# Free head order on ScalarE, a deeper VectorE queue and one wait fewer, in an attention and gated-FFN kernel whose order is planned at build time

## The chip, the cores and the metric

The kernel runs on one core of a Trainium2 chip. The metric is the device time of one execution in microseconds, as the median of several. Executions of one kernel mostly agree within 0.5%. Where two kernels are compared, both ran on the same chip.

## The reference

```python
x = A_x                                            # 1 x 2048 x 512, bf16
g = sigmoid((x * gate_w).sum(-1))                  # one gate per row
a = attention(x, wqkv) @ wo                        # 32 heads of 16 columns, softmax over 2048 keys
b = ((x @ w_gate) * (x @ w_up)) @ w_down           # hidden width 1376
return g * a + (1 - g) * b
```

What matters is the softmax: 32 heads x 2048 x 2048 exponentials. In tiles of 128 keys by 512 queries that is 2048 units of 128x512.

## The kernel before

The program is written by a planner. While it is built, a small model with a clock per engine decides which instruction each engine issues next; the chip then runs the five orders as they were written down, in order on each engine, held together by semaphores. The durations in the model (`dur`, `lat`) decide only the order.

The exponentials are shared by two engines. ScalarE applies `Exp` to two or three units at once, straight from a score tile in PSUM. VectorE takes some row tiles (a key tile of four heads, four units) and makes exponentials of integers: each unit is clipped and evicted from PSUM to int16, and four passes over the 2048 columns then make four terms, whose bit patterns are read as bf16. The fourth pass works in place:

```python
def do_d / d_unit ...                     # eviction: one per unit, PSUM -> int16
    v.tensor_scalar(i2b(nb)[:, j, :], bank, _LO, _HI, ALU.max, ALU.min)
def cheap(e, nb): ...                     # four passes per row tile, k = 0..3
    dstt = LL[:, k, ...] if k < 3 else src
    o = P.op("dve",
        lambda v: v.tensor_scalar(dstt, src, 0.5, _BASE + _OFF[k], ALU.mult, ALU.add),
        pops + ([lf or last_x[0]] if k < 3 else done[:3]),      # k = 3 waits for the other three
        dur=0.6, lat=0.1)
```

PSUM has two score slots, of three and two (later three) banks. A span fills a slot: two or three units for ScalarE, or two for ScalarE and one for VectorE. The slot is free again when ScalarE's exponential and VectorE's eviction are both done.

Two sets of small DMAs go through SyncE's queue, and the planner gives them these times:

```python
# query projection: VectorE evicts it to Qst, eight DMAs spread it into QX
for p in range(2):
    for j in range(4):
        P.dma("sp", ... QX[r0:r0+16, p, b, :] <- Qst[r0:r0+16, s, :] ..., f"dq{s}", dur=0.3)
# normalisation of a block of heads, after its accumulator is copied to oraw
4 x P.dma("sp", ... onum <- oraw ..., f"dnum{s}", dur=0.3)
    P.dma("sp", ... den  <- oraw ..., f"dden{blk % 2}")         # default: dur 0.5, lat 2.2
    P.op("dve", ... rec <- 1 / den ...)
2 x P.dma("sp", ... rscr <- rec ..., f"dscr{s}")
    P.dma("sp", ... rb <- broadcast of rscr ..., "drb")
    P.op("pool", ... OT <- onum * rb ...)                        # read by the output projection
...
n0 = 128 * c + 32 * b - 24        # when a query projection is due, in row tiles
```

The softmax here doesn't subtract the row's maximum and nothing guards it: scores larger than these inputs give would overflow.

Of the kernel before, what the change touches and what calls it, by code (L numbers as in the profile page):

```python
# [151 lines left out]
def _build(nc, A_x, A_wqkv, A_wo, W_gate, W_up, W_down, gate_w, out):  # L152
# [18 lines left out]
    D_LAST = 6  # L171
    D_GAP = 0.3
    D_CHEAP = 5
    D_SLOT = 0.3
    D_IDLE = 0.9
    SLK = 0.15
    KA, VA = 8, 3
# [1 line left out]
    RP = 3  # L179
    DP = 3  # L180
# [9 lines left out]
    with ExitStack() as stack:  # L190
# [242 lines left out]
        last_x = []  # L433
# [317 lines left out]
        pv_done = [0] * NG  # L751
        pv_n = [0] * NG
        on_d = {}
        st = dict(gA=0, actE=None, actJ=0, gD=0, pvg=0, prog=0, i2=0)

        def kq_deps(m, kt):
            c, b, p = grp(m)
            return [ev_k[b, kt // 4 - (b == kt == 0)], q_dma[b, c, p]]

        def act_units(n):  # L760

            r = []
            g, e, j = st["gA"], st["actE"], st["actJ"]
            lf = {g: list(left[g])}
            while len(r) < n:
                if e is None:
                    while g < NG and not lf.setdefault(g, list(left[g])):
                        g += 1
                    if g >= NG:
                        break  # L770
                    e, j = (g, lf[g].pop(0)), 0
                r.append((e, j))
                j += 1
                if j == 4:
                    e = None
            return r

        def take(units):
            for e, j in units:
                if j == 0:  # L780
                    left[e[0]].remove(e[1])
                st["actE"], st["actJ"] = (e, j + 1) if j < 3 else (None, 0)
                st["gA"] = e[0]
                st["prog"] += 1

# [12 lines left out]
        p_ring = []  # L798
# [19 lines left out]
        def backlog(now):  # L818
            return max(0.0, P.t["dve"] - now) + 0.6 * sum(q_[0] < 5 for q_ in dve_q)
# [46 lines left out]
        def do_s(now):  # L866
            r, un, kd, fr = plan_s()
            i = len(spans)
            sl = i % 2

            dj = dh = None
            if len(un) == 3 and spans and not overdue() and backlog(now) < min(need_s() - now, 1.5) + D_SLOT:
                busy = {j for _, j in un[:2]}
                j = d_can(now, busy)
                if j is not None and j not in busy:
                    dj, un, dh = j, un[:2], Hold()
            n = len(un)
            deps = list(kd) + (fr if i >= 2 else o_s3 if i else [])
            if dj is not None:
                deps += kq_deps(*dst["e"])  # L880
                de = dst["e"]
            if un[0][0][0] == NG - 1:
                xs[1]["res"] = True

            def fn(pe):
                q = None
                for k_, ((m, kt), j) in enumerate(all_):
                    c, b, p = grp(m)
                    q = pe.matmul(  # L889
                        bank_ap(sl, k_),  # L890
                        KT[32 * j : 32 * j + 32, b, kt * 128 : (kt + 1) * 128],
                        QX[32 * j : 32 * j + 32, p, b, :],
                        start=True,
                        stop=True,
                        tile_position=(32 * j, 0),
                    )
                return q

            all_ = un + ([(de, dj)] if dj is not None else [])
            o = P.op("pe", fn, deps, "pe_s", dur=MM + 0.01, lat=0.2, mode="s")  # L900
            take(un)
            for (m, kt), j in all_:
                c, b, p = grp(m)
                q_use[b, c] = o
            sp = dict(n=n, slot=sl, units=un, s=o, x=None, h=dh)
            spans.append(sp)
            if dj is not None:
                d_unit(dj, bank_ap(sl, 2), o, dh)
            return {j for _, j in all_}
# [14 lines left out]
        dst = dict(e=None, js=[], buf=0, p1={})  # L924
# [10 lines left out]
        def d_can(now, js_busy):  # L935

            if dst["e"] is None and not d_claim(now):
                return None
            for j in dst["js"]:
                if j not in js_busy:  # L940
                    return j
            return dst["js"][0]

        def d_claim(now):
            if now < D_START or not last_x or tails or l_state["n"] > D_CHEAP:
                return False
            nb = (dst["buf"] + 1) % (3 if "k" in last_v else 2)
            if dst["p1"].get(nb) == "busy":
                return False
            if d_free[nb] is not None and d_free[nb] == "pending":  # L950
                return False
            g = max(st["gD"], st["gA"], 1)
            while g < NG and (not [k for k in DK if k in left[g]] or (g == st["gA"] and len(left[g]) < (D_LAST if g == NG - 1 else D_LEFT))):
                g += 1
            if g >= NG or g > st["gA"] + 1:
                return False
            kt = [k for k in DK if k in left[g]][0]
            if kt not in ev_vd:
                return False
            try:  # L960
                if P.ready(kq_deps(g, kt)) > now:
                    return False
            except KeyError:
                return False
            left[g].remove(kt)
            st["gD"] = g
            dst.update(e=(g, kt), js=[3, 2, 1, 0], buf=nb)
            on_d[g, kt] = nb
            dst["cnt"] = 0
            return True  # L970
# [57 lines left out]
        def cheap(e, nb):  # L1028
            pops = dst["p1ops"].pop(e)
            done = []  # L1030
            l_state["n"] += 4
            l_state["g"] += [e[0]] * 4

            def mk(k):
                lf = l_free[k] if k < 3 else None

                def make():
                    src = i2b(nb)[:, :, :].rearrange("p a b -> p (a b)")
                    dstt = LL[:, k, :, :].rearrange("p a b -> p (a b)") if k < 3 else src
                    o = P.op(  # L1040
                        "dve",
                        lambda v: v.tensor_scalar(dstt, src, 0.5, _BASE + _OFF[k], ALU.mult, ALU.add),  # L1042
                        pops + ([lf or last_x[0]] if k < 3 else done[:3]),
                        dur=0.6,
                        lat=0.1,
                    )
                    done.append(o)
                    l_state["n"] -= 1
                    l_state["g"].remove(e[0])
                    p_op[e, k] = [o]  # L1050
                    p_ring.append((e, k))
                    if k < 3:
                        push_l(k + 1)
                    else:
                        l_state["busy"] = False
                        cheap_kick()

                return make

            def push_l(k):  # L1060
                if k < 3 and l_free[k] == "pending":
                    l_wait[k] = lambda: push_l(k)
                    return
                dve_push(5, pops + [l_free[k] if k < 3 else None], mk(k))
                if k < 3:
                    l_free[k] = "pending"

            cheap_wait.append(lambda: push_l(0))
            cheap_kick()
# [4 lines left out]
        def overdue():  # L1074

            return any(g < st["gA"] for g in l_state["g"])
# [167 lines left out]
        for ch in range(1, NCH):  # L1244
            n0 = 4 * ch - KA
# [3 lines left out]
        for b in range(1, NB):  # L1249
            n0 = 32 * b  # L1250
            fl.append((n0 - 14, mk_q(b, 0, n0 - 14)))
            fl += [(n0 - 12 + 2 * ch, mk_k(b, ch, n0 - 12 + 2 * ch)) for ch in range(NCH)]
        for c in range(1, NCH):
            for b in range(NB):
                n0 = 128 * c + 32 * b - 24
                fl.append((n0, mk_q(b, c, n0)))
        n_ffn = NCH * (2 * FT + 4)
        a0, a1 = FFN_FROM, FFN_TO
# [52 lines left out]
        tails = []  # L1311
# [34 lines left out]
        def step_pe():  # L1346
# [3 lines left out]
            hold = False  # L1350
            if s and s_ready <= t + 0.01 and spans and P.mode == "c":
                fs = [u for u in active if u.pos < len(u.mms)]
                hold = fs and fs[0].mode == "c" and t + fs[0].cost + 0.49 <= need_s() - SLK and need_s() < 1e8
            if s and s_ready <= t + 0.01 and not hold:
                busy = do_s(t)
                xi = x_get(P.t["pe"])
                if xi is not None and (
                    pick_fill(P.t["pe"] + 0.5) is None or any(isinstance(x["u"], Unit) for x in xs)
                ):
                    j = d_can(P.t["pe"], busy)  # L1360
# [4 lines left out]
            pvs = []  # L1365
            if m < NG:
                for it in p_ring:
                    e, k = it
# [8 lines left out]
            fs = [u for u in active if u.pos < len(u.mms)]  # L1377
# [10 lines left out]
            if xi is not None:  # L1388
# [7 lines left out]
                if s_ready > t + D_GAP and backlog(t) < D_IDLE:  # L1396
                    j = d_can(t, set())
# [12 lines left out]
                    return True  # L1410
            pick = None
            nr = sum(q_[1] is None for q_ in pvs)
            if pvs and not hold and (not fs or len(tails) or nr >= RP or len(pvs) - nr >= DP):
                pick = "pv"
            elif fs:
                pick = "f"
            if pick == "pv":
                it = next((q_ for q_ in pvs if (q_[1] is not None) == (nr < RP)), pvs[0])
                p_ring.remove(it)
                do_pv(it)  # L1420
                return True
            if pick == "f":
                u = fs[0]
                k = u.pos
# [180 lines left out]
```

## Time and profile before

The median was 760.57 us. ScalarE is the bound. These are the busy lines of the page: engine, busy us, share of the span and instructions.

```profile
span 759.2 us, 20945 instructions
PE 706.6 (93%) x8946; PEld 213.3 (28%) x8946; DVE 677.7 (89%) x1116; ACT 735.3 (97%) x672; POOL 65.2 (9%) x73
```

The Trainium skill ("Perfetto Trace Analysis", Identifying the Most-Contended Engine) takes occupancy as the measure for Vector and Scalar engines, and warns that it misleads for TensorE. Here the first part fits: ACT is at 97%, and the exponentials follow each other without a gap. The windows view, which gives busy time in a stretch, shows ScalarE at 584 of 585 us between the start-up and the end.

```profile
150.00:735.00 585.00, 550.13 (x6944) 162.41 (x6943) 558.73 (x919) 584.16 (x536) 17.08 (x13) 1.00 0.08 20
```

The columns of this view are: stretch, length, PE, PEld, DVE, ACT and POOL busy with the number of instructions, granted TensorE clock, DMA share, GB/s.

The waits view says who waited for whom, in us in total, times, and the longest:

```profile
ACT PT L1477 <- PE psS L889: 7.2, 15, 0.9
DVE rec L1209 <- DMA den<-oraw: 8.6, 9, 3.1
```

From start to start, an exponential of three units takes 0.4267 x 3 + 0.064 us and one of two 0.4267 x 2 + 0.064 us where nothing stops it. Summed over all exponentials but the last this gives 728.3 us. What the real spacings have beyond that sum I call ScalarE's loss: 11.0 us, of which 8.8 lie before 150 us.

Finally the in-place pause. This is VectorE's timeline around 201 us (start, length, instruction):

```profile
200.96 1.41 DVE L1042 TENSOR_SCALAR SC<-SC 128x2048 int16<-128x2048 int16 x2
202.28 0.68 DVE L1013 TENSOR_SCALAR wk<-psX 128x512 int16<-128x512 f32 x1
202.88 0.68 DVE L1013 TENSOR_SCALAR wk<-psS 128x512 int16<-128x512 f32 x1
```

Instructions follow each other after 0.60 us, but two passes that end in the in-place one take 1.32 us.

### The profile page before, as it was taken

To read this page: it belongs to the slowest core of one execution; us is meant where nothing else is said; L and a number is where in the kernel's file an instruction comes from. 1 tells how busy PE (TensorE), PEld (TensorE's weight loads), DVE (VectorE), ACT (ScalarE), POOL (GpSimd) and SP (SyncE) were. 2 spreads that over 40 slices of the span, in tenths; PEclk is the share of its full clock that TensorE was granted. 3 is DMA by queue.
4 is the path that set the end of the run, shared out by engine and by line. 5 is a ranking of instruction groups with operands and counts; after the bars stand their busy time and mean duration, and the time that the engine had idled before them with its cause. 6 is when DMAs were issued, how large, how long until landed. Compare 5 with 4: busy or idle time off the path is not lost.

```text
span 759.2 us, 20945 instructions
## 1 busy us (share of the span) xinstructions
PE 706.6 (93%) x8946; PEld 213.3 (28%) x8946; DVE 677.7 (89%) x1116; ACT 735.3 (97%) x672; POOL 65.2 (9%) x73
## 2 busy tenths in 40 slices
PE   9998898999899999998999999998999989899997
PEld 3322222222222322222222222222222222222243
DVE  3449987989999999999989989999999989999994
ACT  6989999999999999999999999999999999999995
POOL 8940000000000000000000000000000000000000
PEclk9978898999999999999999999999999999999999
DMA  8900000000010010101001010000001100010000
GB/s 173 284 16 9 16 15 25 16 9 24 9 30 9 23 38 11 29 9 28 12 10 31 29 30 10 24 15 9 24 10 28 40 19 16 7 29 8 24 23 31
DMA packets 32881, 22.81 MB, mean 30 GB/s; under 512 B 20468, under 2 KB 27572, under 8 KB 32788
## 3 DMA queue, kind: packets, MB, share of 16 engines
q1 hardware_dynamic: 31476, 20.42, 10.3%
q8 instruction: 71, 1.16, 0.7%
q0 software_dynamic: 256, 0.79, 0.4%
q10 hardware_dynamic: 1056, 0.26, 0.2%
q14 instruction: 22, 0.18, 0.1%
HBM read 11.24 MB, written 2.35 MB: 18 GB/s over the span
## 4 chain that ended last, share of the span: by engine, by line
ACT 31%; DVE 30%; PE 30%; issue 6%; SPq 1%; DMA 1%; DVEq 0%; ACTq 0%
ACT PT L1477 31%; DVE SC L1042 10%; PE psS L889 9%; DVE SC L1013 9%; PE psX L370 9%; PE psO L1120 8%; DVE wk L1013 4%; PE psS L370 1%; DVE hT L645 1%; DVE usb L632 1%; SPq L1180 1%; DVE wk L1042 1%; DMA den<-oraw 1%; DVE oraw L1173 1%; PE psO L1130 1%
## 5 line engine op out<-in xcount | busy, mean ns | idle before, releaser
L1477 ACT ACTIVATE PT<-psS 128x1024 bf16<-128x1024 f32 (+1 forms) x662 | 727.5, 1286 | 8.7 <-PE psS L889 7.2
L889 PE MATMUL psS<-QX,KT 32*128 32x512 bf16 x1966 | 265.0, 390 | 32.8 <-ACT PT L1477 21.3
L1042 DVE TENSOR_SCALAR SC<-SC 128x2048 int16<-128x2048 int16 x316 | 213.1, 692 | 2.2
L1013 DVE TENSOR_SCALAR SC<-psS 128x512 int16<-128x512 f32 x256 | 172.1, 682 | 15.1 <-PE psS L889 13.0
L1120 PE MATMUL psO<-PT,VV 128*32 128x512 bf16 x1546 | 150.1, 391 | 1.2 <-DVE oraw L1173 0.6
L889 PEld LDWEIGHTS psS<-QX,KT 32*128 32x128 bf16 x1966 | 68.6, 91 | 290.4 <-ACT PT L1477 113.9
L1120 PE MATMUL psO<-SC,VD 128*32 128x512 bf16 x1140 | 106.7, 389 | 4.1 <-DVE SC L1042 3.6
L1233 POOL TENSOR_TENSOR OT<-onum,rb 128x512 bf16<-128x512 f32 x16 | 21.3, 1332 | 674.0 <-DMA rb<-rscr 674.0
L1013 DVE TENSOR_SCALAR wk<-psS 128x512 int16<-128x512 f32 x102 | 68.5, 680 | 1.0 <-PE psS L889 0.7
L1042 DVE TENSOR_SCALAR SC<-wk 128x2048 int16<-128x2048 int16 x93 | 62.1, 688 | 0.1
L1120 PEld LDWEIGHTS psO<-PT,VV 128*32 128x32 bf16 x1546 | 38.6, 95 | 59.0 <-issue 48.2
L370 PE MATMUL psX<-xT,wu 128*32 128x512 bf16 x688 | 53.1, 394 | 1.0 <-DVE SC L1013 0.4
L370 PE MATMUL psX<-wd,hT 128*32 128x512 bf16 (+1 forms) x704 | 52.8, 382 | 0.1
L370 PE MATMUL psX<-xT,wg 128*32 128x512 bf16 x688 | 51.1, 383 | 0.6 <-DVE usb L632 0.2
L1120 PE MATMUL psO<-SC,VV 128*32 128x512 bf16 x428 | 43.3, 395 | 2.6 <-DVE oraw L1173 1.4
L1013 DVE TENSOR_SCALAR SC<-psX 128x512 int16<-128x512 f32 x60 | 40.7, 679 | 2.6 <-PE psX L985 2.6
L1120 PEld LDWEIGHTS psO<-SC,VD 128*32 128x32 bf16 x1140 | 28.1, 95 | 46.7 <-DVE SC L1042 27.2
L645 DVE TENSOR_TENSOR hT<-psX,usb 128x512 bf16<-128x512 f32 (+1 forms) x44 | 29.9, 680 | 3.6 <-PE psX L370 3.5
L985 PE MATMUL psX<-QX,KT 32*128 32x512 bf16 x82 | 32.2, 392 | 0.6 <-DVE hT L645 0.2
L632 DVE CAST usb<-psX 128x512 bf16<-128x512 f32 (+1 forms) x44 | 29.9, 680 | 0.8 <-PE psX L370 0.8
L1042 DVE TENSOR_SCALAR wk<-wk 128x2048 int16<-128x2048 int16 x31 | 21.8, 704 | 0.7
L1173 DVE COPY oraw<-psO 128x512 f32<-128x512 f32 x31 | 21.1, 681 | 0.5 <-PE psO L1120 0.5
(115 smaller groups left out, 363.9 us busy)
## 6 DMA issues: line engine op xcount, KB each, us to landing
rb<-rscr SPq DMA_DIRECT2D x16, 256.0 KB
onum<-oraw SPq DMA_DIRECT2D x124, 32.0 KB, 2.0
QX<-Qst SPq DMA_DIRECT2D x120, 16.0 KB, 1.8
out_dram<-ost SPq DMA_DIRECT2D x12, 128.0 KB, 1.8
wu<-in_B_w_up_dram SPq DMA_DIRECT2D x1, 1376.0 KB, 7.0
wg<-in_B_w_gate_dram SPq DMA_DIRECT2D x1, 1376.0 KB, 9.8
wd<-in_B_w_down_dram SPq DMA_DIRECT2D x1, 1280.0 KB, 12.7
SC<-in_A_x_dram SPq DMA_DIRECT2D x4, 128.0 KB, 3.2
```

Source lines behind the costliest of these rows:

```text
L370: r = pe.matmul(dst_[j : j + 32, :], lhs[:, j : j + 32], rhs, start=s0, stop=s1, tile_position=(0, j), skip_group_check=True,)
L632: "dve", lambda v: v.tensor_copy(usb[0:w, n % 2, :], un.bank[0:w, :]), deps, **EV
L645: lambda v: v.tensor_tensor(hT[0:w, f, :], un.bank[0:w, :], usb[0:w, n % 2, :], ALU.mult),
L889: q = pe.matmul(bank_ap(sl, k_), KT[32 * j : 32 * j + 32, b, kt * 128 : (kt + 1) * 128], QX[32 * j : 32 * j + 32, p, b, :], start=True, st ...
L985: lambda pe: pe.matmul(bank, KT[32 * j : 32 * j + 32, b, kt * 128 : (kt + 1) * 128], QX[32 * j : 32 * j + 32, p, b, :], start=True, stop=True,
L1013: lambda v: v.tensor_scalar(i2b(nb)[:, j, :], bank, _LO, _HI, ALU.max, ALU.min),
L1042: lambda v: v.tensor_scalar(dstt, src, 0.5, _BASE + _OFF[k], ALU.mult, ALU.add),
L1120: r = pe.matmul(psO[r_, :], vcol(m, kt, k_, j), pj, start=first, stop=last, tile_position=(0, 32 * j), skip_group_check=True)
L1130: r = pe.matmul(psO[r_, 256 * hf : 256 * hf + 256] if w < 2 else psD[r_, 0:256], vcol(m, kt, k_, j, hf) if w < 2 else ones[:, k_, 16 - 16 ...
L1173: o_ev[m] = P.op("dve", lambda v: v.tensor_copy(oraw[:, s, :], psO[:]), deps, **EV)
L1233: lambda g: g.tensor_tensor(OT[:, c % 2, b, :], onum[:], rb[:], ALU.mult),
L1477: lambda a: a.activation(cell_ap(cells[0], n).rearrange("p a b -> p (a b)"), bank_ap(sl, 0, n), ACT.Exp, scale=_LN2 / _OCT,),
```

## The change

VectorE's unit rides as the third unit of a score group, and must be another head than ScalarE's two. Before, ScalarE took a tile's heads 0 to 3 in order, so VectorE's head often collided. Now ScalarE may take any two, which leaves VectorE its place more often. The queue allowance (`D_SLOT`) lets a unit go to VectorE although VectorE is busy for longer. The in-place pass no longer waits. Two lesser edits came along: query projections are due 6 row tiles earlier, and the choice of attention-value work counts all finished tiles as pressure.

```diff
-    D_SLOT = 0.3
+    D_SLOT = 0.6
...
-                busy = {j for _, j in un[:2]}
-                j = d_can(now, busy)
-                if j is not None and j not in busy:
-                    dj, un, dh = j, un[:2], Hold()
+                if dst["e"] is not None or d_claim(now):
+                    for j in dst["js"]:
+                        two = act_units(2, j)          # ScalarE's next two, head j taken last
+                        if j not in [j_ for _, j_ in two]:
+                            dj, un, dh = j, two, Hold()
+                            break
...
-                        pops + ([lf or last_x[0]] if k < 3 else done[:3]),
+                        pops + ([lf or last_x[0]] if k < 3 else []),
...
-                n0 = 128 * c + 32 * b - 24
+                n0 = 128 * c + 32 * b - 30
...
-            if pvs and not hold and (not fs or len(tails) or nr >= RP or len(pvs) - nr >= DP):
+            if pvs and not hold and (not fs or len(tails) or press >= RP or len(pvs) - nr >= DP):
```

(`act_units` and `take` keep a list of the heads left; `press` counts all finished ScalarE tiles in the ring, `nr` those whose operands are ready. A second line in which `press` replaces `nr` is left out.)

More of the change, by code (lines that the diff above doesn't have):

```diff
@@ L753, in _build @@
         on_d = {}
-        st = dict(gA=0, actE=None, actJ=0, gD=0, pvg=0, prog=0, i2=0)
+        st = dict(gA=0, actE=None, actJ=[], gD=0, pvg=0, prog=0, i2=0)
         def kq_deps(m, kt):
@@ L758, in kq_deps, with act_units @@
             return [ev_k[b, kt // 4 - (b == kt == 0)], q_dma[b, c, p]]
-        def act_units(n):
+        def act_units(n, but=None):
+            order = lambda js: sorted(js, key=lambda j: (j == but, j))
             r = []
-            g, e, j = st["gA"], st["actE"], st["actJ"]
+            g, e, js = st["gA"], st["actE"], order(st["actJ"])
             lf = {g: list(left[g])}
@@ L770, in act_units @@
                         break
-                    e, j = (g, lf[g].pop(0)), 0
-                r.append((e, j))
-                j += 1
-                if j == 4:
+                    e, js = (g, lf[g].pop(0)), order(range(4))
+                r.append((e, js.pop(0)))
+                if not js:
                     e = None
@@ L779, in take @@
             for e, j in units:
-                if j == 0:
+                if e != st["actE"]:
                     left[e[0]].remove(e[1])
-                st["actE"], st["actJ"] = (e, j + 1) if j < 3 else (None, 0)
+                    st["actE"], st["actJ"] = e, [0, 1, 2, 3]
+                st["actJ"].remove(j)
+                if not st["actJ"]:
+                    st["actE"] = None
                 st["gA"] = e[0]
@@ L1412, in step_pe @@
             nr = sum(q_[1] is None for q_ in pvs)
-            if pvs and not hold and (not fs or len(tails) or nr >= RP or len(pvs) - nr >= DP):
+            press = sum(q_[1] is None for q_ in p_ring)
+            if pvs and not hold and (not fs or len(tails) or press >= RP or len(pvs) - nr >= DP):
                 pick = "pv"
@@ L1417, in step_pe @@
             if pick == "pv":
-                it = next((q_ for q_ in pvs if (q_[1] is not None) == (nr < RP)), pvs[0])
+                it = next((q_ for q_ in pvs if (q_[1] is not None) == (press < RP)), pvs[0])
                 p_ring.remove(it)
```

## The prediction

> **What bounds it now.** ScalarE. The page's busy table gives ACT 735.3 of 759.2 us (97%), DVE 677.7, PE 706.6; the windows view gives ACT 50.00 of 50 in nearly every stretch from 150 to 700 us. In the timeline, exponentials start back to back: from 150 to 600 us a 128x1536 one takes 1.33 us start to start, a 128x1024 one 0.92. The two lengths fit 0.427 us a unit (512 columns) plus 0.064 us an instruction; the 277 wide, 388 narrow and one single-unit instruction then add up to 729 us, against 739 us of actual spacings. The 11 us lost lie at 45 to 150 us (8.4), where the granted clock is 0.74 to 0.93, and near 625 and after 730 us. Dealing fewer units to ScalarE is therefore worth its full duration, as long as PE and DVE keep up. The Trainium skill ("ScalarE: Activation LUTs", What ACT_TABLE_LOAD costs) gives 186 ns + 0.833 ns a column less 93 ns overlap, 946 and 1373 ns here; the trace is slightly quicker and decides.
>
> **What the change moves (built order of both programs).** Row tiles on VectorE rise from 110 to 116. ScalarE loses 24 units: 241 wide (-36) and 430 narrow (+42). That is 42 x 0.917 - 36 x 1.344 = -9.9 us. VectorE gains 24 evictions and 24 2048-wide passes: the timeline spaces both at 0.60 us, so +28.8 us. VectorE heads placed as third head of a score group rise from 358 to 400, lone ones fall from 82 to 64; PE's separate score issues fall by 12, attention-value groups rise by 18 (0.2135 us each) and mode switches fall by 10 (0.105 us): PE is even within a few us.
>
> **In-place set.** In the timeline two passes that end in the in-place one are followed by the next instruction after 1.32 us, not 1.20. About 109 such pauses of 0.12 us lie between 100 and 700 us: 12 us of VectorE. Without the wait most of this returns. The skill's "VectorE: DVE Perf Modes" (The DRAIN you can't avoid) says a semaphore costs nothing extra; here it does, since it waits on the instruction directly in front. VectorE isn't the bound, so this only pays for part of the 28.8 us.
>
> **Critical path.** All of the 9.9 us is on it, but VectorE's slack is used up. Counting the built order per 67 exponentials, VectorE's work at 0.60 us was 65 to 74 us against 71 to 77 of ScalarE's; after it is 68 to 73 against 70 to 73, in three stretches equal or above. The waits view shows that VectorE also loses 8.6 us to the denominators' DMA, in order. The deeper queue (0.3 to 0.6 us) lets evictions finish later, so the bank they hold can reach PE late. I estimate 1 to 3 us of new ScalarE stalls. The start to 45 us and the 9 us after the last exponential stay.
>
> **Prediction:** 752 us (760.6 - 9.9 + about 1.5), 748 to 758 8 times in 10. Faster by over 2% (under 745): 4%; within 2%: 94%; slower: 2%.
>
> **What would show it.** ACT busy about 726 us in 671 exponentials; DVE busy about 705 us in 1164 to 1166 instructions, 95% of the span or more; the 0.12 us pauses gone; from 150 to 700 us ScalarE's spacings within 3 us of 0.427 and 0.064; small new waits of PE's loads on VectorE.
>
> **What would make it wrong.** VectorE saturating so that evictions hold banks and ScalarE stalls by 5 to 10 us, cancelling the gain: then ACT's idle before exponentials grows well above the 8.7 us on the page. Or the new order filling the gaps at 45 to 150 us, worth up to 8 us more.

## The result and the profile after

The changed kernel took 768.97 us (768.81 to 773.14, 4 runs) against 761.04. The ratio is 1.0116, with a 95% interval of 1.0080 to 1.0152. Ratios in this text are the mean time of one kernel's fast runs over that of the other's fast runs of the same rounds, so not quite the ratio of the medians. A run is fast when it lies within 1.5% of the fastest of its kernel; of all runs here one does not (experiment 11).

The first lines are the page's busy lines, the next two are from the waits view:

```profile
span 767.0 us, 21248 instructions
PE 713.1 (93%) x9054; PEld 215.5 (28%) x9054; DVE 701.6 (91%) x1164; ACT 728.9 (95%) x678; POOL 67.4 (9%) x73
...
ACT PT L1484 <- PE psS L895: 19.8, 28, 4.1
DVE rec L1215 <- DMA den<-oraw: 7.9, 10, 3.4
PE psX L370 <- POOL OT L1239: 3.3, 1, 3.3
```

ScalarE did get less to do. Its sum fell from 728.3 to 718.4 us, the 9.9 us that were intended. But its loss rose from 11.0 to 27.4 us. The span adds up from the profiled executions as follows.

| us | before | after |
|---|---|---|
| start to first exponential | 10.6 | 10.3 |
| ScalarE's sum (all but the last exponential) | 728.3 | 718.4 |
| its loss before 150 us | 8.8 | 8.4 |
| its loss from 150 to 735 us | 1.6 | 18.2 |
| its loss after 735 us | 0.6 | 0.8 |
| end of the last exponential to the end | 8.7 | 10.2 |
| span (with the last exponential) | 759.2 | 767.0 |

The new loss has two parts. About 10 us lie in two places: 4.7 us between 398 and 407 us and 5.3 us between 592 and 602 us. The rest is in some two dozen gaps, most of 0.15 to 0.7 us, the longest of 1.24 us at 494 us. The first place, as the chain that ended last shows it (start, length, what):

```profile
396.69 0.23 SPq L1186
396.96 0.59 SPq L1186
...
398.86 1.88 DMA den<-oraw
400.74 0.02 issue
400.77 0.35 DVE rec L1215
```

SyncE issues DMAs, one lands, and VectorE's reciprocal starts 3.42 us after VectorE last worked. VectorE runs in order, so every eviction behind that reciprocal waits too. The timeline of SyncE's queue tells why the DMA was late. After:

```profile
390.52 5.76 SPq L509 DMA_DIRECT2D QX<-Qst  x8
396.33 2.48 SPq L1186 DMA_DIRECT2D onum<-oraw  x4
398.86 0.60 SPq L1196 DMA_DIRECT2D den<-oraw  x1
401.15 1.17 SPq L1223 DMA_DIRECT2D rscr<-rec  x2
403.73 0.64 SPq L1236 DMA_DIRECT2D rb<-rscr  x1
```

The same block before:

```profile
392.25 2.43 SPq L1180 DMA_DIRECT2D onum<-oraw  x4
394.73 0.60 SPq L1190 DMA_DIRECT2D den<-oraw  x1
397.02 1.17 SPq L1217 DMA_DIRECT2D rscr<-rec  x2
399.60 0.64 SPq L1230 DMA_DIRECT2D rb<-rscr  x1
406.63 5.69 SPq L509 DMA_DIRECT2D QX<-Qst  x8
```

Eight query DMAs hold the queue for 5.76 us, and after the change they stand in front of the normalisation's DMAs instead of behind them. Line 509 belongs to the query projection, which is due 6 row tiles earlier: a block of heads lasts 32 row tiles, so a projection that is due 30 ahead comes 2 row tiles after the block before its own has begun, which is while the block before that one is normalised. Over the whole trace the eight DMAs stand between the accumulator's copy and the reciprocal's broadcast in 8 of 16 blocks (in one of them, seven of the eight), and in none before. The chain at the second place has the same cause. There the queries sit in front of the `rscr` and `rb` DMAs, GpSimd's multiply comes 17.0 us after the start of the accumulator's copy instead of about 12, and TensorE, which runs in order, stands at the output projection until it is done. First SyncE's queue, then the chain:

```profile
580.46 0.60 SPq L1196 DMA_DIRECT2D den<-oraw  x1
582.24 5.38 SPq L509 DMA_DIRECT2D QX<-Qst  x8
587.66 1.21 SPq L1223 DMA_DIRECT2D rscr<-rec  x2
590.28 0.64 SPq L1236 DMA_DIRECT2D rb<-rscr  x1
```

```profile
590.28 3.89 DMA rb<-rscr
...
594.33 1.56 POOL OT L1239
595.89 0.09 issue
595.98 1.90 PE psX L370 x16
597.88 0.54 PE psS L895 x3
```

ScalarE starves meanwhile (its timeline):

```profile
591.02 3.38 ACT L1484 ACTIVATE PT<-psS 128x1024 bf16<-128x1024 f32 x3
598.53 1.45 ACT L1484 ACTIVATE PT<-psS 128x1536 bf16<-128x1536 f32 x1 [4.13 <-PE psS L895]
```

Each stall also comes with a slower clock. The windows view gives the granted TensorE clock as 0.50 behind the first stall and from within the second, for 3.4 and 6.8 us by the trace's clock records:

```profile
403.40:406.80 3.40, 3.29 (x26) 0.65 (x26) 3.14 (x6) 2.09 (x3) 0.00 (x0) 0.50 0.24 82
596.00:601.40 5.40, 5.40 (x45) 1.23 (x45) 1.78 (x3) 2.38 (x2) 0.00 (x0) 0.50 0.08 27
```

The Trainium skill ("TensorE: Matmul & The Clock Gate", Part 1: The HAM clock gate) says that TensorE falls to half rate after an idle window of about 3.4 us. The trace agrees only in part. Half rate does come with TensorE's two longest waits, but these are 2.90 and 3.30 us, and the second time half rate began at 594.56 us, when TensorE had stood for only 1.88 us.

### The profile page after: what moved, and what is told of

The parts are those of the page before. It is cut to its first block, busy times and chain, and to the rows that moved or that the text cites. A ratio compares the mean times of both kernels' runs of the same rounds, so it can differ in the third digit from the quotient of the medians.

```text
span 767.0 us, 21248 instructions
## 1 busy us (share of the span) xinstructions
PE 713.1 (93%) x9054; PEld 215.5 (28%) x9054; DVE 701.6 (91%) x1164; ACT 728.9 (95%) x678; POOL 67.4 (9%) x73
## 4 chain that ended last, share of the span: by engine, by line
DVE 40%; PE 28%; ACT 20%; issue 4%; SPq 3%; DMA 3%; POOL 1%; DVEq 0%; POOLq 0%; ACTq 0%
ACT PT L1484 20%; DVE SC L1048 15%; DVE SC L1019 12%; PE psS L895 9%; PE psX L370 8%; PE psO L1126 7%; DVE wk L1019 5%; SPq L1186 3%; DVE usb L632 2%; DMA den<-oraw 2%; DVE hT L645 2%; DVE oraw L1179 1%; DVE wk L1048 1%; PE psO L1136 1%; PE psS L370 1%
## 5 line engine op out<-in xcount | busy, mean ns | idle before, releaser
L895 PE MATMUL psS<-QX,KT 32*128 32x512 bf16 x1984 | 271.8, 390 | 28.3 <-ACT PT L1484 15.5
L1048 DVE TENSOR_SCALAR SC<-SC 128x2048 int16<-128x2048 int16 x332 | 219.4, 701 | 0.8 <-PE psO L1126 0.4
L1019 DVE TENSOR_SCALAR SC<-psS 128x512 int16<-128x512 f32 x284 | 190.2, 686 | 13.7 <-PE psS L895 12.2
L1126 PE MATMUL psO<-SC,VD 128*32 128x512 bf16 x1208 | 113.4, 391 | 6.5 <-DVE SC L1048 5.8
L1019 DVE TENSOR_SCALAR wk<-psS 128x512 int16<-128x512 f32 x116 | 77.9, 687 | 0.9 <-PE psS L895 0.8
L1048 DVE TENSOR_SCALAR SC<-wk 128x2048 int16<-128x2048 int16 x99 | 69.0, 717 | 0.6 <-PE psO L1126 0.5
L370 PE MATMUL psX<-wd,hT 128*32 128x512 bf16 (+1 forms) x704 | 56.1, 386 | 0.2 <-DVE bsb L683 0.2
L1019 DVE TENSOR_SCALAR SC<-psX 128x512 int16<-128x512 f32 x48 | 32.9, 686 | 1.3 <-PE psS L895 1.2
L991 PE MATMUL psX<-QX,KT 32*128 32x512 bf16 x64 | 25.4, 398 | 1.4 <-DVE usb L632 0.6
L1179 DVE COPY oraw<-psO 128x512 f32<-128x512 f32 x31 | 21.3, 687 | 0.9 <-PE psO L1126 0.9
```

The source lines that it names most:

```text
L370: r = pe.matmul(dst_[j : j + 32, :], lhs[:, j : j + 32], rhs, start=s0, stop=s1, tile_position=(0, j), skip_group_check=True,)
L895: q = pe.matmul(bank_ap(sl, k_), KT[32 * j : 32 * j + 32, b, kt * 128 : (kt + 1) * 128], QX[32 * j : 32 * j + 32, p, b, :], start=True, st ...
L991: lambda pe: pe.matmul(bank, KT[32 * j : 32 * j + 32, b, kt * 128 : (kt + 1) * 128], QX[32 * j : 32 * j + 32, p, b, :], start=True, stop=True,
L1019: lambda v: v.tensor_scalar(i2b(nb)[:, j, :], bank, _LO, _HI, ALU.max, ALU.min),
L1126: r = pe.matmul(psO[r_, :], vcol(m, kt, k_, j), pj, start=first, stop=last, tile_position=(0, 32 * j), skip_group_check=True)
L1179: o_ev[m] = P.op("dve", lambda v: v.tensor_copy(oraw[:, s, :], psO[:]), deps, **EV)
```

## The experiments

Two theories were set against each other. Theory Q: the query DMAs in SyncE's queue are the cause, through a planner that believes in 0.3 us a DMA where the trace shows 0.6. Theory D: VectorE has no slack left, so that any delay reaches ScalarE. Some kernels keep the order of every engine as it was planned and alter one thing afterwards; these are clean. The others are planned anew, and a new plan puts all small collisions in other places.

The record marks every result as correct, also that of experiment 10, whose arithmetic is cut short.

### 1. Query DMAs behind the normalisation, order kept

```diff
+        for each rb DMA: take the query DMAs planned up to 6 us before its block's
+        onum DMAs or since, and move them behind it in SyncE's order
         P.emit(nc, stack)
```

> The changed kernel with every engine's order kept except SyncE's: the eight query DMAs that stood between the last accumulator copy of a block and its reciprocal's broadcast are issued after that broadcast. Theory Q (the earlier query projection puts its eight DMAs, 0.6 us each, in front of the normalisation's DMAs in SyncE's queue; one of these delays stops VectorE 3.4 us at 401 us and another stops TensorE 3.3 us at 596 us, together about 10 us of ScalarE's stalls): 757 to 761 us, multiply at about +12 us after the copy in every block, no stall of ScalarE over 1.5 us after 150 us. Theory D (VectorE simply has no slack left, so the stalls would come anyway): 767 to 769 us.

Measured: 760.86 us, ratio 1.0010 (0.9983 to 1.0036). The changed kernel's was 1.0116, so 8 us came back (by the two intervals, give or take 3). Both stalls are gone, no denominator is waited for longer than 1.1 us, and the multiply comes 11.9 to 13.5 us after the copy in every block:

```profile
ACT PT L1484 <- PE psS L895: 12.7, 21, 1.0
DVE rec L1215 <- DMA den<-oraw: 4.6, 10, 1.1
```

Theory Q accounts for the 8 us. But the time only equals the kernel before. ScalarE's loss from 150 to 735 us is still 10.8 us, against 1.6 before. (This profile is of the slowest of four executions, 2.5 us above the median, so 10.8 is on the high side.)

### 2. Queries due 24 ahead again, planned anew

```diff
-                n0 = 128 * c + 32 * b - 30
+                n0 = 128 * c + 32 * b - 24
```

> The changed kernel with the query projections due 24 row tiles ahead again, not 30; the order is planned anew (116 row tiles on VectorE as in the changed kernel). Theory Q: 755 to 760 us, no query DMA inside the normalisation's DMAs. Theory D: 766 us or more.

Measured: 767.41 us, ratio 1.0112. Theory Q's range missed; by the number alone it is theory D's. The trace shows another cause. No query DMA stands inside the normalisation any more, but in this plan a projection comes too late: TensorE waits for its DMAs, and ScalarE loses 4.3 us between 295 and 299 us. This is presumably what the edit to 30 was made against.

```profile
PE psS L895 <- DMA QX<-Qst: 2.4, 1, 2.4
```

### 3. Queue allowance back at 0.3, planned anew

> The changed kernel with VectorE's queue allowance back at 0.3; planned anew (113 row tiles on VectorE, ScalarE's sum 724 us against 719). Theory Q: the collisions with the query DMAs stay, 765 us or more. Theory D: VectorE gets slack back and the time falls to 757 to 760 us.

Measured: 780.15 us, ratio 1.0266. It refutes theory D as the whole cause: VectorE had less to do, and the time rose. VectorE now waits 26.7 us for denominators, up to 5.3 us at a time, and the query DMAs stand before the denominator's in three blocks. The other waits, the longest among them, have no query DMA in front: there the plan puts the reciprocal right or soon behind the accumulator's copy, and the denominators land 5 us or more after the copy starts. That is a third way to lose time, which neither theory names.

```profile
DVE rec L1215 <- DMA den<-oraw: 26.7, 11, 5.3
```

### 4. The kernel before with queries due 30 ahead, planned anew

> The kernel before with the query projections due 30 row tiles ahead, nothing else; planned anew (108 row tiles on VectorE, ScalarE's sum 732 us against 729). Theory Q: query DMAs inside the normalisation of several blocks, 765 to 772 us. Theory D: 763 to 764 us, ScalarE's 3 us alone, because VectorE still has its slack.

Measured: 778.81 us (771.66 to 783.11), ratio 1.0212: slower than either range. The profiled execution was the slowest of four. One edited number costs the kernel before more than the whole change did, and query DMAs stand inside the normalisation in 9 of 16 blocks: one wait of 3.1 us for GpSimd comes with them. There are also 21.3 us of waits for denominators, and 24 us of half clock between 130 and 745 us, against 3.4 before. But only one of the seven waits for a denominator over 0.5 us has query DMAs in front. The other six are of the third kind of experiment 3, so this run shows that the earlier due date brings the collisions, and not that they alone cost the 2%.

### 5. The kernel before without the in-place wait, order kept

> The kernel before, every engine's order kept, only the in-place pass's wait taken away (its dependence on the three passes that read the same tile first is dropped after planning; VectorE runs them in order). About 109 pauses of 0.12 us of VectorE should vanish. If VectorE has slack in the kernel before: 759.5 to 760.6 us, no gain. If it were already co-critical: 752 to 757 us.

Measured: 760.42 us, ratio 1.0006 (0.9974 to 1.0037). No gain. The pauses are gone: the two passes that took 1.32 us above now take 1.20.

```profile
203.53 1.28 DVE L1042 TENSOR_SCALAR SC<-SC 128x2048 int16<-128x2048 int16 x2
204.73 0.68 DVE L1013 TENSOR_SCALAR wk<-psX 128x512 int16<-128x512 f32 x1
```

Counting them properly showed an error of the prediction. The in-place pass pauses only where it stands directly behind the third pass, 64 times with a median of 0.117 us, 7.3 us in all. Where another instruction stands between (43 times) the pause is nil. Most of the other pauses that the prediction had counted are still there without the wait.

### 6. The repaired changed kernel with the in-place wait put back, order kept

> The repaired changed kernel (query DMAs behind the normalisation), every order kept, with the in-place wait put back: 116 pauses of 0.12 us, 13 us more of VectorE. Theory D (what is left of the new stalls of ScalarE is VectorE without slack): 6 to 13 us slower than the repaired kernel, 766 to 773 us. If the remaining stalls come from elsewhere: 760 to 763 us.

Measured: 766.65 us, ratio 1.0085 (1.0064 to 1.0106), beside 1.0010 for the repaired kernel: about 5.7 us more, give or take 3 by the two intervals. The pauses are 72 and take 8.3 us. (The profiled execution was the fastest of six, so its trace shows less than that.) The same 7 to 8 us of VectorE cost nothing measurable in the kernel before (give or take 2.4 us) and by the median most of their length here. That is theory D at work, at the lower edge of what was expected.

### 7 and 8. Planned with the DMA times of the trace

```diff
-    query and onum DMAs: dur=0.3         (lat 2.2)
+    query and onum DMAs: dur=0.62, lat=1.3 and 1.4
-    den, rscr, rb DMAs:  dur=0.5, lat=2.2
+    den: dur=0.6, lat=1.35;  rscr: dur=0.6, lat=1.3;  rb: dur=0.64, lat=3.3
```

> The changed kernel, planned with the times that the trace shows for SyncE's DMAs (0.62 us of queue each where the planner had 0.3 or 0.5, and their landing), nothing else; 115 row tiles on VectorE. Theory Q with an honest planner: no wait of VectorE for a denominator over 1 us, no wait of TensorE on GpSimd; 753 to 760 us. If VectorE's lack of slack rules: 760 to 766 us.

> The kernel before, planned with the DMA times that the trace shows; 111 row tiles on VectorE, ScalarE's sum 1 us smaller. 757 to 760 us by theory Q, which leaves the kernel before little to gain, as its query DMAs already miss the normalisation's.

Measured: the changed kernel so planned takes 756.05 us, ratio 0.9944 (0.9921 to 0.9966), and beats both kernels. The kernel before so planned takes 761.47, ratio 1.0014: slightly above its expectation, and no gain. Each is one new plan, and experiments 9, 11 and 12 are plans with the same times that gain nothing, so how much of the 0.6% is due to the times and how much to a lucky plan is not shown. In the changed one ScalarE's loss from 150 to 735 us is 7.4 us, and one wait for a denominator is 1.3 us, where none over 1 us was expected:

```profile
ACT PT L1490 <- PE psS L896: 8.1, 19, 1.1
DVE rec L1219 <- DMA den<-oraw: 1.3, 1, 1.3
```

### 9. Planned with the DMA times, queries due 24 ahead

> The changed kernel with queries due 24 ahead again and the planner given the DMA times of the trace; 115 row tiles on VectorE as in the version with the times and 30 ahead (756 us). With the earlier rerun of 24 ahead (767 us) TensorE stood 2.4 us at 294 us for query DMAs that the planner thought landed. Theory Q (wrong DMA times in the plan are the cause, and 24 or 30 only decides where they hit): 754 to 759 us with no wait of TensorE on query DMAs. If 30 ahead is itself what helps: 762 us or more.

Measured: 764.01 us, ratio 1.0051. It missed: 30 ahead itself helps here. From 291 to 297 us TensorE has no score group to issue, as the next queries have not landed, and ScalarE stands for 4.0 us. So in these two plans 30 is the better due date once the planner has the DMA times. VectorE also waits 3.1 and 2.6 us for two denominators here, again with no query DMA in front.

### 10. VectorE relieved, order kept, result wrong on purpose

```diff
+                    cut = 512 if k == 2 and len(on_d) > 4 else 2048     # third pass made short
-    v.tensor_scalar(dstt, src, ...)
+    v.tensor_scalar(dstt[:, 0:cut], src[:, 0:cut], ...)
```

The starting point is the repaired kernel of experiment 1. The in-place wait is back.

> A wrong result on purpose. The repaired changed kernel (query DMAs behind the normalisation, every order kept), in which the third 2048-wide pass of each row tile after the first few is cut to 512 columns, and the in-place wait is put back because the check asks for it: some 45 us less of VectorE's passes, 8 us more of pauses. Theory D (what is left of the new stalls is VectorE without slack): ScalarE runs at the sum of its durations outside the start, 749 to 753 us. If the stalls have another cause (TensorE, the clock): 757 to 761 us.

Measured: 754.54 us, ratio 0.9921 (0.9886 to 0.9955), 6.8 us under the repaired kernel by the ratios, give or take 3. It lies between the two ranges, 1.5 us above theory D's, but the gain itself is what theory D foretold: only VectorE's work was cut, and TensorE was as busy as before. The windows of the repaired kernel and, in the second fence, of the relieved one:

```profile
150.00:735.00 585.00, 551.65 (x6923) 161.34 (x6920) 573.45 (x946) 577.99 (x540) 17.42 (x13) 1.00 0.08 20
```

```profile
150.00:735.00 585.00, 552.14 (x7093) 163.99 (x7093) 553.93 (x956) 582.11 (x548) 17.72 (x14) 1.00 0.08 20
```

VectorE falls from 98.0% to 94.7% of the stretch, about where it was before the change (95.5%), and ScalarE rises from 578.0 to 582.1 us of 585. ScalarE's total loss is 11.7 us, within 1 us of the kernel before. (This profile is of the fastest of four executions, that of the repaired kernel of the slowest, so the ratio is the better measure.) So with enough slack on VectorE some 6 us of the 9.9 show in the time (0.9921). Part of what remains of the gap is the end: 10.2 us behind the last exponential instead of 8.7.

### 11 and 12. With the DMA times, one part undone

> The changed kernel planned with the DMA times of the trace (756 us), VectorE's queue allowance back at 0.3; 113 row tiles on VectorE, ScalarE's sum 4 us larger, VectorE's work 7 us smaller. If the deeper queue pays for itself: 757 to 761 us. If it costs as much in stalls as it gains: 754 to 757 us.

> The changed kernel planned with the DMA times of the trace (756 us), but with ScalarE taking the heads in fixed order as before; 112 row tiles on VectorE, ScalarE's sum 6 us larger than with the free order. If the free order is what gives the gain: 759 to 762 us, no better than the kernel before. If it is not needed: 755 to 757 us.

Measured: allowance 0.3 takes 771.41 us, ratio 1.0116, which missed by 10 us. One execution of six, the profiled one, took 1441 us with every matmul at about half rate; it is left out of the ratio. Fixed order takes 763.61, ratio 1.0026: 1.6 us above its range. Beside 0.9944 the free order is worth about 6 us, and in this plan the other edits gain nothing without it.

### 13 to 16. What was still open

> The same program as e11_slot03_dmatimes, run again for a profile in the normal state. 765 to 773 us again. If VectorE's slack were all that matters, it should have been faster than the version with allowance 0.6 (7 us less of VectorE's work); so the profile must show stalls of ScalarE from TensorE or the queries: windows of half clock in number, or TensorE waiting for query or normalisation DMAs.

> The changed kernel planned with the DMA times of the trace, every order kept except that SyncE issues the query DMAs behind the normalisation's. If the collisions that remain in 7 blocks cost time though they are planned for: 751 to 755 us. If a planned collision is harmless: within 1 us of the repeat in this call, about 755 to 757 us.

> The changed kernel planned with the DMA times of the trace, with the attention-value choice as in the kernel before (only tiles whose operands are ready count as pressure); 116 row tiles on VectorE, ScalarE's sum within 1 us of the other's. If that hunk matters: 3 us or more either way; if not: 754 to 759 us.

> A repeat of e7_after_dmatimes: 754 to 758 us, 0.4 to 0.8% under the kernel before.

The repeat of experiment 7 on another chip took 756.86 us, ratio 0.9941 (0.9914 to 0.9968): confirmed. With the query DMAs moved behind the normalisation as well it took 756.05, ratio 0.9938: the planned collisions cost nothing that these runs can tell. With the old attention-value choice it took 758.95, ratio 0.9970 (0.9944 to 0.9995). The two intervals overlap, so that edit is worth 2 us or nothing. Allowance 0.3 again took 771.14 us, ratio 1.0124. Its profiled execution, at 766 us of span, is the fastest of four. ScalarE loses 12.9 us from 150 to 735 us, and VectorE waits 11.7 us for denominators, against 1.3 us in experiment 7:

```profile
DVE rec L1219 <- DMA den<-oraw: 11.7, 6, 4.4
```

The longest of these waits, 4.4, 3.8 and 2.7 us, end at 260, 671 and 624 us. No query DMA stands in front of them: they are of the third kind of experiment 3, with the reciprocal at most two instructions behind the accumulator's copy. The two spells of half clock (6.8 us each) begin at 260 and 673 us, beside the first two. So waits in VectorE's order are one candidate for the slower time; whether they account for it was not tested.

VectorE's busy share alone does not settle it either. With allowance 0.3 VectorE is busy for 95.5% of the stretch from 150 to 735 us, like the kernel before, and ScalarE loses 12.9 us; with the query DMAs moved behind the normalisation (the second of these four, run 14) it is 98.4%, more than in the repaired kernel, and ScalarE loses only 5.4.

## Why the prediction was wrong

- **The bound and the gain were right.** ScalarE's exponentials are the 241 and 430 predicted, and its sum fell by the 9.9 us computed. ACT busy is 728.9 us (predicted 726) and DVE busy 701.6 us in 1164 instructions (predicted 705 in 1164 to 1166).
- **The step that failed is "I estimate 1 to 3 us of new ScalarE stalls".** They were 16.4 us (27.4 less 11.0): about 8 us from the order of SyncE's queue, which the estimate left out, and most of the rest from VectorE's load, which it set too low. The prediction named the danger, VectorE's saturation with stalls of 5 to 10 us, but as an outside chance.
- **About half of the stalls came from an edit that was not costed at all.** The prediction did not mention that queries are due 6 row tiles earlier. Moving their DMAs back in SyncE's queue, all orders kept, returned 8 us. The prediction had quoted the denominators' waits of 8.6 us from the page, but took them as a number that stays. It did not ask what else goes through that queue.
- **Most of the other half is VectorE's slack, mis-sized.** The prediction compared VectorE's work with ScalarE's and found both about equal, "in three stretches equal or above", and yet allowed 1 to 3 us. The repaired kernel loses 10.8 us from 150 to 735 us at 98.0% VectorE, and 4.8 us when VectorE is relieved to 94.7%; by the ratios the relief gained 6.8 us. In this order of instructions, 98.0% was already too much. It is no threshold: another order lost less at 98.4% (run 14).
- **"About 109 pauses ... 12 us" was an overcount.** They were 64 and 7.3 us. All VectorE pauses of that length had been put down to the in-place pass without checking which instruction stood before each. That the wait costs at all, and that taking it away gains nothing where VectorE isn't the bound, was right.
- **"95% of the span or more" for DVE was wrong** (91%), and did not follow from the prediction's own numbers: 705 of 752 us is 94%. The busy time itself came out right, and the longer span lowered the share. A share over the whole span hides saturation; from 150 to 735 us the repaired kernel had 98.0%.
- **The end grew by 1.5 us**, which the prediction had held constant. This was not tested.

## What to carry to other kernels

When a planned, in-order program is changed, cost every edit, also a due date: ask what each moved instruction shares a queue with. Give a planner's model the measured issue time of small DMAs: with them this change gained 0.6% instead of losing 1.2%. But other plans with the same times came out up to 1.2% slower than the kernel before, so every new plan has to be measured. And before work is moved to the engine that is second in line, test its slack: with every order kept, 8.3 us of pauses on VectorE cost the repaired kernel about 5.7 us, while 7.3 us of them cost the kernel before nothing measurable.

## What the Trainium skill lacked or had wrong

- "DMA: Bandwidth & Descriptors", Issuing engines are not separate DMA queues, calls the sequencer's time to start a DMA "usually small relative to the DMA itself". Here a query DMA of 16 KB held SyncE's queue for 0.59 us (median of 120) and landed 1.8 us after its issue; eight in a row held it for 5.76 us, and that queue time was the cause of 8 us.
- "VectorE: DVE Perf Modes", The DRAIN you can't avoid, finds that a semaphore after each instruction costs nothing extra. It does not treat a wait on the instruction directly in front: that paused VectorE for 0.117 us (64 times before, 72 in experiment 6), and for nothing with one instruction between.
- "TensorE: Matmul & The Clock Gate", Part 1, gives an idle window of about 3.4 us as the condition for half rate; the page's section on PSUM-queue cycling allows for shorter gaps, without a figure. In the repaired kernel the clock was halved from 689.0 to 692.4 us although TensorE's matmuls were busy for 2.30 of the 3.40 us before, as the windows view shows (the stretch before, and the one at half clock; the ends of matmuls are modelled in this view):

```profile
685.60:689.00 3.40, 2.30 (x29) 0.72 (x28) 3.40 (x6) 3.40 (x4) 0.00 (x0) 1.00 0.00 0
689.00:692.40 3.40, 3.40 (x27) 0.90 (x24) 2.14 (x5) 2.41 (x3) 0.00 (x0) 0.50 0.17 39
```

- No page tells of a trace with a busy TensorE and no clock record at all. "TensorE: Matmul & The Clock Gate", Part 1, warns only that clock events in a trace can be unreliable. One execution of experiment 11 took 1439.7 us from first to last instruction, with score matmuls at a mean of 662 ns instead of 391. Its trace has no clock record, where the other traces have 6 to 28, so the clock of 1.00 that is listed for it was not measured. Its cause stays open. The same program ran normally in nine other executions.
